# A written-out order per engine from step 31 on, and ten of the float64 tiles moved beside the attention

## The chip, the cores and the metric

One core of a Trainium2 chip. Times are device microseconds (us). The engines are called as the profile calls them: PE (TensorE, with its weight load PEld), DVE (VectorE), ACT (ScalarE), POOL (GpSimd) and SP (SyncE, which issues most transfers).

## What is computed

Landmark attention, then a gated layer, then a layer with PReLU (the reference, shortened; 576 positions, 8 heads of 64, batch 4, 32 landmarks):

```python
A, Bm, C = sm(q, k_lm), sm(q_lm, k_lm), sm(q_lm, k)      # softmax; _lm: means of 18 rows
Z = Bm.transpose(0, 1, 3, 2) / (norm1(Bm) * norminf(Bm) + 1e-06)
for _ in range(6):
    Z = 2 * Z - Z @ Bm @ Z
x = (A @ Z @ C @ v)                                      # as 2304 tokens x 512
x = (sigmoid(x @ w_gate) * (x @ w_val)) @ w_out          # 512 -> 1536 -> 512
h = x @ w_in2
out = (maximum(h, 0) + alpha * minimum(h, 0)) @ w_out2   # 512 -> 2048 -> 512
```

The weights come as float64. The kernel turns them into float32 on the chip.

## The kernel before

**Products.** A float32 product is made of three matmuls: each factor is split into a rounded high part and the remainder (`split`: a cast on ACT, L129, and a subtraction, L130, on DVE, or on POOL where asked for).

**The gated layer** runs in 96 steps, `at = 24*b + i`, over batches b, halves of 288 tokens and the 12 slices f of 128 of the 1536 features. A step first issues `layer1`: 12 matmuls into two banks `gv` (L716), a sigmoid on ACT (L727), a multiplication on DVE (L728), and the split of the result into `gs` (cast L129, subtraction L130). Then it issues `layer2` (L735, 12 matmuls into four banks `acc`) of the step two before it (`LAG`, `catch_up`). After the last f of a half the four banks are copied out (`xs`, L928) and stored to `x2d`. The attention of batches 1 to 3 is cut into pieces (`later_attentions`) that are issued between these steps, and its result is folded into the weights (`fold`, steps 19 to 55); those of batch 3 are stored (`we3d`) and fetched again by `take_stored`, two at every second step from step 61 on, through two buffers `st`.

**Float64 tiles.** The weights of the last layer are 32 tiles of 128 x 512 float64 (512 KB). `narrow_w2` loads one into `raw2` and makes float32 of it by integer operations on its halves: `scale` on ACT (L154), then `low` on ACT (L158, even tiles) or a shift on DVE (L160, odd tiles), then two joins on DVE (L163, L166), of which the second writes the tile `n2`; that is stored to `w2d`. From step 53 on it is called once per 0.9 step (`NARROW_EVERY`). There are two `raw2` buffers and one `n2` buffer. The first two tiles run early; 30 run in the steps from 57 on.

**The final stage** follows step 95: pairs of seven products (`prod`, L1024) and the output layer (`o`, L1068). Its inputs are `x7`, made from `x2d` by `load_x`, `sums_x` (L849) and `make_x7`. For the first group of tokens eight parts of them are issued together at step 74 and six at step 83 (`X2_AT`).

**What sets the order.** Each engine runs its own queue in order. The order of a queue is made ahead of time from the order in which the code issues operations, with priorities (`tc.high_priority`), by a scheduler. Nothing in the kernel before fixes it by hand, except `behind_of`, which puts one instruction behind another in this ordering.

Of the kernel before, what the change touches and what calls it, by code (L numbers as in the profile page):

```python
# [21 lines left out]
def tile_landmark_attention_glu_prelu(  # L22
# [45 lines left out]
    X2_AT, W2_AT = (74, 83), (88, 91)  # L68
# [7 lines left out]
    NARROW_FROM, NARROW_EVERY = 53, 0.9  # L76
# [58 lines left out]
    narrowed = [None]  # L135

# [7 lines left out]

    def raw_tile(name):
        return wpool.tile([P, NW], U64, tag="raw", name=name, bufs=4)

    def narrow(raw, to=None, act=False):
# [17 lines left out]
        narrowed[0] = nc.vector.scalar_tensor_tensor(  # L166
# [3 lines left out]
        return w[:, :, 0]  # L170
# [536 lines left out]
    def layer1(b, half, f):  # L707
# [19 lines left out]
        nc.scalar.activation(g, pss[0][:, :HB], AF.Sigmoid)  # L727
        nc.vector.tensor_tensor(out=g, in0=g, in1=pss[1][:, :HB], op=ALU.mult)  # L728
        split(gs, g)
# [71 lines left out]
    def narrow_w2(i):  # L801

        f, which = divmod(i, 2)
        pool = rpool or apool
        raw = pool.tile([P, NW], U64, tag="raw2", name="raw2", bufs=2)
        if which == 0:
            nc.sync.dma_start(
                out=raw.rearrange("p (a c) -> p a c", a=NK),
                in_=w_in2[:, P * f : P * f + P].rearrange("(a p) c -> p a c", p=P),
            )  # L810
        else:
            nc.sync.dma_start(out=raw, in_=w_out2[P * f : P * f + P, :])
        t = pool.tile([P, NW], F32, tag="n2", name="n2", bufs=1)
        narrow(raw, t, act=which == 0)
# [33 lines left out]
    def sub(out, x, y):  # L848
        nc.vector.tensor_tensor(out=out, in0=x, in1=y, op=ALU.subtract)  # L849

    def sums_x(i):
        b11, b12, b22, t1, t2 = (xf[i][n] for n in ((0, 0), (0, 1), (1, 1), "T1", "T2"))
        sub(t1, b12, b11)
        sub(t2, b22, t1)

        sub(b12, b22, b12)

    def make_x7(i, op, kk):
        if i == 0 and (op, kk) == (6, 0):
            sums_x(i)  # L860
# [9 lines left out]
        split(t, src[:, kk])  # L870
# [29 lines left out]
    part = {}  # L900
    to_narrow = deque(range(2 * NF2))
# [5 lines left out]
    behind = deque()  # L907
# [24 lines left out]
    for b in range(B):  # L932
# [5 lines left out]
        for i, (half, f, f0, f1) in enumerate(order):  # L938
            at = 24 * b + i
            behind.append((b, half, f, f0, f1, layer1(b, half, f)))  # L940
# [47 lines left out]
            if at == X2_AT[1]:
                assert not to_narrow
# [174 lines left out]
```

## Time and profile before

| | |
|---|---|
| median of 3 runs | 871.6 us (867.6 to 872.51) |
| the profiled execution: its own time | 870.5 us |
| its span | 868.7 us |
| mean granted TensorE clock | 0.976 of full speed |
| PE busy | 814.9 us (94%), x6017 |
| PEld busy | 712.6 us (82%) |
| DVE busy | 579.4 us (67%), x1205 |
| ACT busy | 468.1 us (54%), x982 |
| POOL busy | 68.9 us (8%), x70 |

All stages together share one execution; the span is the time from its first to its last instruction, and the execution's own time adds what lies around it. The gated layer's steps take up the time to 483 us, the final stage the rest. A share of busy time is an average over stages with different limits, so the stretches are read apart below.

### The profile page before, as it was taken

The page shows a single profiled execution, that of the slowest core. Times are in us where ns is not written, and L with a number is a line of the kernel's source. Part 1 is how long each engine was busy: PE and PEld are TensorE (multiplying, and loading weights), DVE is VectorE, ACT ScalarE, POOL GpSimd, SP SyncE. Part 2 cuts the span into 40 slices and gives each one's busy share as a digit, 9 for nine tenths or more (in the row PEclk, how much of TensorE's full clock was granted, in tenths as well). Part 3 has the DMA queues.
Part 4 walks back from the last instruction along what each step waited for, and adds up shares of the span by engine and source line. Part 5 has one row for each costly group of instructions (what it writes and reads, how often), then busy time and mean ns, then how long its engine had stood idle before and what let it go on. Part 6 is the DMA issues. An engine that isn't in the chain of part 4 may idle for free.

```text
span 868.7 us, 15870 instructions
## 1 busy us (share of the span) xinstructions
PE 814.9 (94%) x6017; PEld 712.6 (82%) x6017; DVE 579.4 (67%) x1205; ACT 468.1 (54%) x982; POOL 68.9 (8%) x70
## 2 busy tenths in 40 slices
PE   5688889999999999987999899999999999999996
PEld 4366667777889878987999798988989989989895
DVE  2799998666573444778686788889554568645544
ACT  6766785466452344556454556556444356444443
POOL 0131223111110100340000000000000000000000
PEclk9779999999999999998999999999999999999999
DMA  9768787864312344777687464576643345652002
GB/s 251 260 198 242 237 270 212 226 179 124 79 42 98 126 145 149 244 248 252 228 246 243 174 242 146 197 246 216 189 135 112 104 147 182 203 185 98 1 1 72
DMA packets 98604, 150.99 MB, mean 174 GB/s; under 512 B 37328, under 2 KB 58336, under 8 KB 98528
## 3 DMA queue, kind: packets, MB, share of 16 engines
q1 hardware_dynamic: 95072, 137.40, 50.1%
q0 software_dynamic: 3456, 12.58, 4.6%
q8 instruction: 47, 0.77, 0.4%
q14 instruction: 29, 0.24, 0.1%
HBM read 108.01 MB, written 41.94 MB: 173 GB/s over the span
## 4 chain that ended last, share of the span: by engine, by line
PE 68%; DMA 10%; DVE 10%; ACT 5%; issue 4%; POOL 2%; SPq 1%; DVEq 0%; ACTq 0%; POOLq 0%
PE o L1068 23%; PE prod L1024 20%; PE gv L716 9%; PE acc L735 9%; DMA raw<-in_moe_w_in_dram 3%; DMA w2d<-n 2%; PE psf L675 2%; DVE raw L163 2%; PE psq L215 1%; DVE n L166 1%; DMA raw<-in_moe_w_out_dram 1%; ACT raw L158 1%; DMA raw<-in_moe_w_val_dram 1%; PE psc L238 1%; PE psa L238 1%
## 5 line engine op out<-in xcount | busy, mean ns | idle before, releaser
L1024 PE MATMUL prod<-x,w 128*128 128x384 f32 x1008 | 199.8, 337 | 1.6 <-ACT p L1092 1.6
L716 PE MATMUL gv<-A,we 128*128 128x288 f32 x1152 | 190.5, 308 | 10.5 <-DVE g L728 3.8
L1024 PEld LDWEIGHTS prod<-x,w 128*128 128x128 f32 x1008 | 180.3, 188 | 14.5 <-ACT p L1092 1.9
L716 PEld LDWEIGHTS gv<-A,we 128*128 128x128 f32 x1152 | 164.0, 193 | 32.8 <-issue 16.6
L735 PE MATMUL acc<-gs,wconv 128*128 128x288 f32 x1152 | 181.0, 302 | 9.8 <-DVE gs L130 4.8
L1068 PE MATMUL o<-w,g2s 128*128 128x512 f32 x693 | 180.4, 393 | 0.0
L735 PEld LDWEIGHTS acc<-gs,wconv 128*128 128x128 f32 x1152 | 162.1, 191 | 18.2 <-DVE gs L130 6.9
L1068 PEld LDWEIGHTS o<-w,g2s 128*128 128x128 f32 x693 | 128.3, 188 | 19.9 <-DVE g2s L130 0.3
L1038 ACT ACTIVATE n<-h 128x384 f32<-128x384 f32 x96 | 50.4, 525 | 90.8 <-DVE h L1085 90.0
L1040 DVE SCALAR_TENSOR_TENSOR h<-n,minus_alpha,h 128x384 f32<-128x384 f32 x96 | 59.1, 617 | 53.8 <-ACT h L1039 53.5
L129 ACT CAST gs<-g 128x288 fp32r<-128x288 f32 x96 | 41.3, 431 | 62.3 <-DVE g L728 61.8
L728 DVE TENSOR_TENSOR g<-g,gv 128x288 f32<-128x288 f32 x96 | 43.1, 449 | 32.7 <-PE gv L716 29.1
L129 ACT CAST g2s<-h 128x384 fp32r<-128x384 f32 x77 | 39.4, 513 | 44.9 <-DVE h L1040 44.9
L163 DVE SCALAR_TENSOR_TENSOR raw<-raw 128x512 uint32<-128x512 uint32 x68 | 52.0, 777 | 14.3 <-ACT raw L158 13.0
L727 ACT ACTIVATE g<-gv 128x288 f32<-128x288 f32 x96 | 39.3, 409 | 39.8 <-PE gv L716 38.9
L154 ACT ACTIVATE raw<-raw 128x512 f32<-128x512 f32 x68 | 45.8, 681 | 27.3 <-DMA raw<-in_moe_w_out_dram 12.2
L130 DVE TENSOR_TENSOR gs<-g,gs 128x288 fp32r<-128x288 f32 x96 | 47.3, 493 | 18.4 <-ACT gs L129 18.0
L1085 DVE TENSOR_TENSOR h<-u,prod 128x384 f32<-128x384 f32 x72 | 39.8, 553 | 26.1 <-PE prod L1024 22.9
L1039 ACT ACTIVATE h<-h 128x384 f32<-128x384 f32 x96 | 50.4, 525 | 2.7
L130 DVE TENSOR_TENSOR g2s<-h,g2s 128x384 fp32r<-128x384 f32 x77 | 42.7, 556 | 11.0 <-ACT g2s L129 9.4
L1068 PE MATMUL o<-w,g2r 128*128 128x512 f32 x171 | 45.2, 393 | 0.0
L1068 PEld LDWEIGHTS o<-w,g2r 128*128 128x128 f32 x171 | 31.7, 188 | 5.1
(160 smaller groups left out, 836.1 us busy)
## 6 DMA issues: line engine op xcount, KB each, us to landing
w<-w7d SPq DMA_DIRECT2D x48, 512.0 KB, 3.6
raw<-in_moe_w_out_dram SPq DMA_DIRECT2D x28, 512.0 KB, 5.2
wgv<-wgvd POOLq DMA_DIRECT2D x24, 512.0 KB, 4.5
w7d<-w SPq DMA_DIRECT2D x24, 512.0 KB, 3.0
raw<-in_moe_w_in_dram SPq DMA_DIRECT2D x16, 512.0 KB, 4.4
w2d<-n SPq DMA_DIRECT2D x32, 256.0 KB, 2.6
raw<-in_moe_w_gate_dram SPq DMA_DIRECT2D x24, 256.0 KB, 4.0
raw<-in_moe_w_val_dram SPq DMA_DIRECT2D x24, 256.0 KB, 4.4
```

What stands on the lines that cost most here:

```text
L129: nc.scalar.copy(dst[:, 0, :], src)
L130: (nc.gpsimd if lo == "pool" else nc.vector).tensor_tensor(out=dst[:, 1, :], in0=src, in1=f32(dst[:, 0, :]), op=ALU.subtract)
L154: nc.scalar.activation(w[:, :, 1], w[:, :, 1], AF.Copy, scale=2.0 ** -112)
L163: nc.vector.scalar_tensor_tensor(out=lo, in0=hi, scalar=0x80000000, in1=lo, op0=ALU.bitwise_and, op1=ALU.bitwise_or)
L716: nc.tensor.matmul(ps[:, :HB], lhsT=We[b, c, j][:, a, 256 * i + P * s : 256 * i + P * s + P], rhs=att[b, j, "A"][half][:, e, :], start=(n ...
L728: nc.vector.tensor_tensor(out=g, in0=g, in1=pss[1][:, :HB], op=ALU.mult)
L735: nc.tensor.matmul(acc[m][:, :HB], lhsT=wout_sb[f][:, a, P * m : P * m + P], rhs=gs[:, e, :], start=(f == f0 and n == 0), stop=(f == f1 - ...
L1024: nc.tensor.matmul(ps[:, :HG], lhsT=w[:, a, kk], rhs=x7[i, op, kk][:, e], start=(n == 0), stop=(n == 5),)
L1038: nc.scalar.activation(n, h, AF.Relu, scale=-1.0)
L1039: nc.scalar.activation(h, h, AF.Relu)
L1040: nc.vector.scalar_tensor_tensor(out=h, in0=n, scalar=minus_alpha[:, f : f + 1], in1=h, op0=ALU.mult, op1=ALU.add)
L1068: nc.tensor.matmul(acc, lhsT=gs[:, a, P * t : P * t + P], rhs=w2_out[f][:, e, :], start=(count[i, u] == 1 and k == 0), stop=(count[i, u] = ...
```

## The change

- Ten of the 30 tiles get places at steps 34, 36, ... 52, and 20 at steps 58, 59, 60, 62, ... 85 (`NARROW_AT`). The first two are made at step 30's place in the code, at a priority that puts them where they were.
- From step 31 on (`PIN_FROM`) `layer1` issues the operations of a step, those of the tile among them, in a written-out order, and `pin` puts each behind the one that was pinned before it on the same engine. That fixes the order in the queue and adds no wait. The order is: shift (odd tiles), sigmoid, scale, multiplication, cast, subtraction, low (even tiles), joins. The store of a tile and the load of a later one are issued one step after it, behind the subtraction.
- Buffers: from step 56 on three for `raw2` (one of its own, two of tag A) and two for `n2`.
- `we3` is fetched one per step at steps 58 to 69, and taken one per step (`load_stored`, `take_stored`).
- The parts of `x7` of the first group are made one per step, eight from step 75 and six from step 88, with the subtraction on POOL; the three sums of `xf` stand at steps 77, 78 and 79.

```diff
-    X2_AT, W2_AT = (74, 83), (88, 91)
+    X2_AT, W2_AT = (74, 87), (88, 91)
-    NARROW_FROM, NARROW_EVERY = 53, 0.9
+    NARROW_FROM, NARROW_AHEAD, PIN_FROM, PIN_POOL = 30, -2000, 31, 56
+    NARROW_AT = {*range(34, 53, 2), *(58 + 29 * i // 20 for i in range(20))}
+    def pin(ins):
+        e = ins.ins.engine
+        if e in pinned:
+            behind_of(ins, pinned[e])
+        pinned[e] = ins
+        return ins
-    def take_stored(c):
-        for j in range(2):
-            st = rpool.tile([P, NW], F32, tag="st3", name="st3", bufs=2)
-            nc.sync.dma_start(out=st, in_=we3d[c, j])
-            We[B - 1, c, j] = ws_tile("we3")
-            split(We[B - 1, c, j], st, lo="pool")
+    def load_stored(c, j):
+        st = rpool.tile([P, NW], F32, tag="st3", name="st3", bufs=2)
+        pin(nc.sync.dma_start(out=st, in_=we3d[c, j]))
+        stored.append((c, j, st))
+    def take_stored():
+        c, j, st = stored.popleft()
+        We[B - 1, c, j] = t = ws_tile("we3")
+        pin(nc.scalar.copy(t[:, 0, :], st))
+        nc.gpsimd.tensor_tensor(out=t[:, 1, :], in0=st, in1=f32(t[:, 0, :]), op=ALU.subtract)
...
+        tile_ = loaded.popleft() if at in NARROW_AT else None
+        if tile_ is not None and tile_[0] % 2:
+            pin(narrow_shift(tile_[1]))
+        pin(nc.scalar.activation(g, pss[0][:, :HB], AF.Sigmoid))
+        if tile_ is not None:
+            pin(narrow_scale(tile_[1]))
+        pin(nc.vector.tensor_tensor(out=g, in0=g, in1=pss[1][:, :HB], op=ALU.mult))
+        pin(nc.scalar.copy(gs[:, 0, :], g))
+        rest = pin(
+            nc.vector.tensor_tensor(
+                out=gs[:, 1, :], in0=g, in1=f32(gs[:, 0, :]), op=ALU.subtract
+            )
+        )
+        if to_store:
+            i, t = to_store.popleft()
+            load_w2(rest)
+            behind_of(pin(nc.sync.dma_start(out=w2d[i], in_=t)), rest)
+        if tile_ is not None:
+            i, raw = tile_
+            if i % 2 == 0:
+                pin(narrow_low(raw))
+            t = (rpool or apool).tile([P, NW], F32, tag="n2", name="n2", bufs=2 if rpool else 1)
+            for ins in narrow_join(raw, t):
+                pin(ins)
+            to_store.append((i, t))
...
+        if rpool is None:
+            raw = apool.tile([P, NW], U64, tag="raw2", name="raw2", bufs=2)
+        elif i % 3:
+            raw = bpool.tile([P, NW], U64, tag="A", name="raw2", bufs=4)
+        else:
+            raw = rpool.tile([P, NW], U64, tag="raw2", name="raw2", bufs=1)
...
-        split(t, src[:, kk])
+        note(nc.scalar.copy(t[:, 0, :], src[:, kk]))
+        note(
+            (nc.gpsimd if i == 0 else nc.vector).tensor_tensor(
+                out=t[:, 1, :], in0=src[:, kk], in1=f32(t[:, 0, :]), op=ALU.subtract
+            )
+        )
...
-            if at >= NARROW_FROM:
-                narrow_pace += 1 / NARROW_EVERY
-                while to_narrow and narrow_pace >= 1:
-                    narrow_w2(to_narrow.popleft())
-                    narrow_pace -= 1
+            if at in (PIN_FROM, PIN_POOL):
+                for _ in range(2 if at == PIN_FROM else 3):
+                    load_w2(pinned[mybir.EngineType.DVE])
             if at == X2_AT[0]:
                 load_x(0)
-                for op, kk in PARTS7[:8]:
-                    make_x7(0, op, kk)
+                x2_todo = deque(PARTS7[:8])
+            elif x2_todo:
+                op, kk = x2_todo.popleft()
+                if op in (2, 6) and (op, kk) != (6, 1):
+                    pin(sum_x(0, 2 * (op == 6) + kk))
+                make_x7(0, op, kk, pin)
```

The order of DVE's queue at step 34, where the attention of batches 2 and 3 runs (`kT`, `qT`: its keys and queries; `psa`, `ta`: its scores). Before:

```order
L728 TENSOR_TENSOR g<-g,gv_3270 128x288
L130 TENSOR_TENSOR gs<-g,gs 128x288
L221 TENSOR_REDUCE kT_3298<-kT_3298 128x32
L221 TENSOR_REDUCE qT_3313<-qT_3313 128x32
L388 STREAM_TRANSPOSE ta<-psa_3358 128x512
```

The same place of the changed kernel (L770 is the multiplication, L773 the subtraction, L183 and L185 are the joins):

```order
L770 TENSOR_TENSOR g<-g,gv_3290 128x288
L773 TENSOR_TENSOR gs<-g,gs 128x288
L183 SCALAR_TENSOR_TENSOR raw_3130<-raw_3130 128x512
L185 SCALAR_TENSOR_TENSOR n_3305<-raw_3130 128x512
L246 TENSOR_REDUCE kT_3323<-kT_3323 128x32
L246 TENSOR_REDUCE qT_3338<-qT_3338 128x32
L413 STREAM_TRANSPOSE ta<-psa_3386 128x512
```

The two joins of a tile now stand between the step's subtraction and the reduction of kT.

DVE's queue at step 36, at the start of the Newton iterations that run there (`srz`, `psz`: its matrices; `cv`, `at`, `A`: the attention beside it). Before:

```order
L416 STREAM_TRANSPOSE at<-ta 128x576
L516 TENSOR_TENSOR srz<-sbt 128x4x32
L130 TENSOR_TENSOR gs<-g,gs 128x288
L130 TENSOR_TENSOR A_3534<-at,A_3534 128x288
L511 TENSOR_TENSOR srz<-psbb,sbt 128x4x32
L130 TENSOR_TENSOR A_3537<-at,A_3537 128x288
L512 TENSOR_TENSOR srz<-eye,srz 128x4x32
L361 TENSOR_SCALAR cv<-psv,rd 128x64
L529 TENSOR_TENSOR srz<-srz,psz 128x4x32
```

The changed kernel:

```order
L773 TENSOR_TENSOR gs<-g,gs 128x288
L541 TENSOR_TENSOR srz<-sbt 128x4x32
L183 SCALAR_TENSOR_TENSOR raw_3132<-raw_3132 128x512
L441 STREAM_TRANSPOSE at<-ta 128x576
L536 TENSOR_TENSOR srz<-psbb,sbt 128x4x32
L185 SCALAR_TENSOR_TENSOR n_3451<-raw_3132 128x512
L537 TENSOR_TENSOR srz<-eye,srz 128x4x32
L386 TENSOR_SCALAR cv<-psv,rd 128x64
L131 TENSOR_TENSOR A_3570<-at,A_3570 128x288
L131 TENSOR_TENSOR A_3573<-at,A_3573 128x288
L554 TENSOR_TENSOR srz<-srz,psz 128x4x32
```

The two joins stand inside the chain of srz, the tile's shift some rows ahead of these, and the two subtractions for A have moved behind it. On PE the first psz group of this chain, which stood behind three matmuls of a gv group, now stands behind seven.

ACT's queue at steps 66 to 68 (L727 sigmoid, L129 cast, L154 scale, L158 low). Before:

```order
L727 ACTIVATE g<-gv_5007 128x288
L129 CAST gs<-g 128x288
L154 ACTIVATE raw_4815<-raw_4815 128x512
L129 CAST we_5171<-st_5169 128x512
L727 ACTIVATE g<-gv_5047 128x288
L129 CAST gs<-g 128x288
L154 ACTIVATE raw_4859<-raw_4859 128x512
L158 ACTIVATE raw_4859<-raw_4859 128x512
L129 CAST we_5176<-st_5174 128x512
L727 ACTIVATE g<-gv_5097 128x288
```

The changed kernel (L767 sigmoid, L771 cast, L165 scale, L170 low, L733 the cast of `we3`):

```order
L767 ACTIVATE g<-gv_5046 128x288
L165 ACTIVATE raw_4940<-raw_4940 128x512
L771 CAST gs<-g 128x288
L170 ACTIVATE raw_4940<-raw_4940 128x512
L733 CAST we_5086<-st_5002 128x512
L767 ACTIVATE g<-gv_5091 128x288
L771 CAST gs<-g 128x288
L733 CAST we_5126<-st_5044 128x512
L767 ACTIVATE g<-gv_5131 128x288
L165 ACTIVATE raw_4984<-raw_4984 128x512
```

Scale has moved ahead of its step's cast, and not every step has one.

## Rows read from the trace of the kernel before

**Rows 1.** PE timeline, undisturbed: start us, length us, engine, line, operation, out<-in, count
```profile
416.80 1.74 PE L716 MATMUL gv<-A,we 128*128 128x288 f32 x12
418.38 1.75 PE L735 MATMUL acc<-gs,wconv 128*128 128x288 f32 x12
```

**Rows 2.** PE timeline, step 57 to the first prod; in brackets idle time before, its releaser
```profile
340.17 1.74 PE L716 MATMUL gv<-A,we 128*128 128x288 f32 x12
...
405.06 1.49 PE L735 MATMUL acc<-gs,wconv 128*128 128x288 f32 x9 [2.55 <-ACT xs L928]
...
408.11 3.08 PE L716 MATMUL gv<-A,we 128*128 128x288 f32 x12
...
481.57 1.86 PE L735 MATMUL acc<-gs,wconv 128*128 128x288 f32 x12 [0.42 <-DVE gs L130]
...
483.26 2.25 PE L1024 MATMUL prod<-x,w 128*128 128x384 f32 x12
```

**Rows 3.** Windows: span, busy us of PE, PEld, DVE, ACT, POOL, PEclk, DMA share, GB/s
```profile
230.00:285.00 55.00, 54.07 (x723) 49.48 (x722) 28.77 (x85) 24.18 (x60) 5.66 (x7) 1.00 0.22 66
285.00:340.00 55.00, 55.00 (x498) 42.97 (x498) 23.78 (x46) 21.28 (x46) 2.64 (x5) 1.00 0.37 123
340.00:483.00 143.00, 133.81 (x961) 130.50 (x960) 104.55 (x198) 76.95 (x167) 17.34 (x12) 0.98 0.75 243
374.00:414.00 40.00, 33.12 (x209) 30.76 (x208) 31.51 (x56) 21.85 (x48) 8.56 (x6) 0.91 0.79 250
```

**Rows 4.** Waits, 340 to 483: us in total, times, longest us
```profile
ACT raw L154 <- DMA raw<-in_moe_w_out_dram: 12.2, 8, 3.1
ACT raw L154 <- DMA raw<-in_moe_w_in_dram: 11.0, 9, 3.1
...
DVE n L166 <- DMA w2d<-n: 5.5, 9, 1.2
```

**Rows 5.** ACT timeline at one late load
```profile
392.54 0.68 ACT L154 ACTIVATE raw<-raw 128x512 f32<-128x512 f32 x1 [3.12 <-DMA raw<-in_moe_w_in_dram]
...
393.66 0.39 ACT L727 ACTIVATE g<-gv 128x288 f32<-128x288 f32 x1
...
394.88 0.43 ACT L129 CAST gs<-g 128x288 fp32r<-128x288 f32 x1 [0.82 <-DVE g L728]
```

**Rows 6.** Lines, 340 to 483: count, busy us, mean ns, idle before
```profile
L158 ACT ACTIVATE raw<-raw 128x512 uint32<-128x512 uint16 x15 | 9.9, 658 | 0.0
...
L160 DVE TENSOR_SCALAR raw<-raw 128x512 uint32<-128x512 uint32 x15 | 6.4, 425 | 7.0 <-DMA raw<-in_moe_w_out_dram 7.0
...
L129 ACT CAST we<-st 128x512 fp32r<-128x512 f32 x12 | 7.4, 627 | 2.6 <-DMA st<-we3d 2.4 <-PE gv L716 0.2
...
L130 POOL TENSOR_TENSOR we<-st,we 128x512 fp32r<-128x512 f32 x12 | 17.3, 1459 | 61.7 <-ACT we L129 57.0 <-PE acc L735 4.7
...
L849 DVE TENSOR_TENSOR xf<-xf 128x768 f32<-128x768 f32 x4 | 3.8, 950 | 0.0
```

**Rows 7.** DMA issues, 340 to 480: KB each, median us to landing
```profile
raw<-in_moe_w_in_dram SPq DMA_DIRECT2D x14, 512.0 KB, 4.4
...
st<-we3d SPq DMA_DIRECT2D x12, 256.0 KB, 3.7
```

**Rows 8.** POOL and DVE timelines while POOL runs and behind it
```profile
384.04 2.98 POOL L130 TENSOR_TENSOR we<-st,we 128x512 fp32r<-128x512 f32 x2 [3.11 <-ACT we L129]
...
384.31 0.46 DVE L728 TENSOR_TENSOR g<-g,gv 128x288 f32<-128x288 f32 x1
...
385.81 1.52 DVE L130 TENSOR_TENSOR gs<-g,gs 128x288 fp32r<-128x288 f32 x1
...
387.77 0.69 DVE L163 SCALAR_TENSOR_TENSOR raw<-raw 128x512 uint32<-128x512 uint32 x1
```

**Rows 9.** DVE timeline at step 34
```profile
242.40 0.46 DVE L130 TENSOR_TENSOR gs<-g,gs 128x288 fp32r<-128x288 f32 x1 [0.50 <-ACT gs L129]
243.98 0.75 DVE L221 TENSOR_REDUCE kT<-kT 128x32 f32<-128x576 f32 x1 [1.12 <-ACT kT L220]
```

More of the change, by code (lines that the diff above doesn't have):

```diff
@@ L169, in narrow @@
         )
-        return w[:, :, 0]
+    def narrow(raw, to=None, act=False):
+        narrow_scale(raw)
+        (narrow_low if act else narrow_shift)(raw)
+        narrowed[0] = narrow_join(raw, to)[1]
+        return words(raw)[0][:, :, 0]
     att = {}
@@ L726, in layer1 @@
         gs = bpool.tile([P, 2, HB], F32R, tag="gs", name="gs", bufs=GS_BUFS)
[L727 to L729 removed]
+        if at < PIN_FROM:
+            nc.scalar.activation(g, pss[0][:, :HB], AF.Sigmoid)
+            nc.vector.tensor_tensor(out=g, in0=g, in1=pss[1][:, :HB], op=ALU.mult)
+            split(gs, g)
+            return gs
+        tile_ = loaded.popleft() if at in NARROW_AT else None
[23 more added lines that the diff above has]
+            to_store.append((i, t))
         return gs
@@ L799, in make_w2_out, with load_w2 @@
             split(w2_out[2 * g + i], t[:, i])
-    def narrow_w2(i):
-        f, which = divmod(i, 2)
-        pool = rpool or apool
-        raw = pool.tile([P, NW], U64, tag="raw2", name="raw2", bufs=2)
+    loaded, to_store = deque(), deque()
+    def load_w2(after=None):
+        if not to_narrow or (rpool is None and after is not None and to_narrow[0] >= EARLY):
+            return
+        i = to_narrow.popleft()
+        f, which = divmod(i, 2)
+        if rpool is None:
[4 more added lines that the diff above has]
+            raw = rpool.tile([P, NW], U64, tag="raw2", name="raw2", bufs=1)
         if which == 0:
-            nc.sync.dma_start(
+            ins = nc.sync.dma_start(
                 out=raw.rearrange("p (a c) -> p a c", a=NK),
@@ L811, in narrow_w2 @@
         else:
-            nc.sync.dma_start(out=raw, in_=w_out2[P * f : P * f + P, :])
-        t = pool.tile([P, NW], F32, tag="n2", name="n2", bufs=1)
-        narrow(raw, t, act=which == 0)
+            ins = nc.sync.dma_start(out=raw, in_=w_out2[P * f : P * f + P, :])
+        if after is not None:
+            behind_of(pin(ins), after)
+        loaded.append((i, raw))
+    def narrow_w2():
+        load_w2()
+        i, raw = loaded.pop()
+        t = apool.tile([P, NW], F32, tag="n2", name="n2", bufs=1)
+        narrow(raw, t, act=i % 2 == 0)
         nc.sync.dma_start(out=w2d[i], in_=t)
@@ L848, in sub, with sum_x, make_x7 @@
     def sub(out, x, y):
-        nc.vector.tensor_tensor(out=out, in0=x, in1=y, op=ALU.subtract)
+        return nc.vector.tensor_tensor(out=out, in0=x, in1=y, op=ALU.subtract)
+    def sum_x(i, n):
+        b11, b12, b22, t1, t2 = (xf[i][m] for m in ((0, 0), (0, 1), (1, 1), "T1", "T2"))
+        return sub(*((t1, b12, b11), (t2, b22, t1), (b12, b22, b12))[n])
     def sums_x(i):
[L852 to L860, printed above, removed]
+        for n in range(3):
+            sum_x(i, n)
+    def make_x7(i, op, kk, note=lambda ins: ins):
         b11, b12, b21, b22, t1, t2 = (
@@ L900, in tile_landmark_attention_glu_prelu @@
     part = {}
+    EARLY = 12
     to_narrow = deque(range(2 * NF2))
@@ L906, in tile_landmark_attention_glu_prelu @@
     accs = {}
-    behind = deque()
+    behind, x2_todo = deque(), None
     def catch_up():
@@ L939, in tile_landmark_attention_glu_prelu @@
             at = 24 * b + i
-            behind.append((b, half, f, f0, f1, layer1(b, half, f)))
+            behind.append((b, half, f, f0, f1, layer1(at, b, half, f)))
             if len(behind) > LAG:
```

53 lines of the change are left out of this document (33 added, 20 removed).

## The prediction

> **What bounds the kernel now.** I read the busy shares first: TensorE (PE) is at work for 94% of the span, so only what makes PE wait can move the time. Next I took PE's timeline where nothing disturbs it [rows 1]: a step is one gv group and one acc group of 12 matmuls, and groups start 1.58 to 1.59 us apart, so a step takes 3.17 us. Then I took the stretch from gv of step 57, at 340.17, to the first prod of the final stage, at 483.26 [rows 2]: 143.1 us for 39 gv groups and 41 acc groups (468 and 493 records of 12 each). At 1.585 us each they need 80 x 1.585 = 126.8. So **16.3 us are lost there**, and that is the ceiling of any gain in this stretch. Rows 2 show the kind of loss: acc waits 2.55 us at 405.06 (the four acc banks are copied out late, because the engines that copy are late), and .42 for gs at 481.57. Soon behind the wait of 405 a gv group takes 3.08 us instead of 1.74; the granted clock over 374 to 414 is 0.91 [rows 3], so part of the time is paid after the wait, at PE's lower level of 1.2 GHz.
>
> Who is late? The table of waits [rows 4]: ScalarE (ACT) stands at L154, the first operation on a float64 tile, for 12.2 + 11.0 us, for the two kinds of loads, and VectorE (DVE) at L166 for 5.5 us until the single n2 buffer is stored. ACT runs in order, so its queue stands with it: at 392.54 it waits 3.12 us for raw, and the sigmoid L727 starts only at 393.66, behind scale and low [rows 5]. The reason is the pace: 30 tiles are asked for every 0.9 step (2.85 us), while a load takes 4.4 us to land [rows 7] and there are two buffers for it.
>
> Last I looked for room. From 285 to 340 PE is busy 55.00 of 55.00 us, DVE 23.8 and ACT 21.3; from 230 to 285 it is 54.07, 28.8 and 24.2 [rows 3]. So beside the attention DVE has 57 us free of 110.
>
> **The change, part by part.**
>
> *Ten tiles move to steps 34 to 52.* A tile costs ACT .68 (scale) and, if even, .66 (low); DVE .42 (shift) if odd, and two joins. The durations are in rows 5 and 6, and a join that nothing stretches takes .69 [rows 8]. Ten tiles: DVE 20 x .69 + 5 x .42 = 15.9 us, ACT 10 x .68 + 5 x .66 = 10.1. Cover: DVE 57 us free, ACT 110 - 45.5 = 64 [rows 3]. Their loads have room too (DMA share .22 and .37). So in bulk they cost nothing. If that cover did not exist, each tile would put 2.6 us on PE's path (the last rival).
>
> They do stand in fixed places. At step 34 the two joins now stand ahead of the kT reduce. Before, gs ends its subtraction at 242.40 + .46 and the reduce starts at 243.98 [rows 9]. The cast ends by 242.40, low (.66) by 243.06, two joins (1.38) by 244.44, so the reduce is about .4 late, and PE's next psa products with it. At step 36 two joins and a shift (1.80) stand inside the Newton chain, and two subtractions of A (.92) moved behind it, and PE does four matmuls more of gv in between (.53): 1.80 - .92 - .53 = .35 (a matmul is 1.585 / 12 = .132). The other eight tiles meet fewer attention operations; I estimate .45 for them together. Sum **+1.2**; bounds 0 (PE has gv matmuls to fill with) and 3.9 (the same stalls, with the clock's lower level behind them for two groups, as at 408: 2 x (3.08 - 1.74) = 2.7 more).
>
> *Twenty tiles over steps 58 to 85.* One per 1.45 steps, 4.6 us. With a landing of 4.4 [rows 7] and three raw buffers, a load leaves at the latest behind the next step's subtraction and is first used two to three steps later: 6.34 us allowed, so 1.9 to spare. Two n2 buffers: a store has 1.45 steps more than the old one, which cost 5.5 us of DVE waits. Per step DVE has at most .46 + .46 + 1.38 + .42 = 2.72 us, ACT .41 + .68 + .43 + .66 + .63 = 2.81, both under 3.17 (mult and gs in rows 8 and 9, sigmoid and cast in rows 5, we3's cast in rows 6). So no engine is over its step, on average or at worst.
>
> *Fixed order.* Sigmoid now stands ahead of scale, so a late tile no longer delays g; it delays the cast behind it. From the start of a gv group gs is ready after 1.59 (the group) + .3 + .46 (multiplication) + .5 + .46 (subtraction), about 3.3 us, the .3 and .5 being as the idles of rows 9; the acc group that reads it runs two steps later and starts 5 groups after, at 7.92. **Slack 4.6 us** per step. All the single waits on raw of rows 4 are at most 3.1 long: such a wait, if it came, would be swallowed.
>
> *we3 one per step* (before, two at every second step): cast .63 [rows 6], POOL subtraction 1.46, landing 3.7 [rows 7], 5.8 us around two buffers that are asked for every two steps, 6.34. It fits by .5.
>
> *x7 of group 0: eight parts at steps 75 to 82 and six at 88 to 93, one each, subtraction on POOL (GpSimd) instead of DVE.* Fourteen subtractions leave DVE. But rows 8 show what POOL does to DVE: while POOL runs, from 384.04 to 387.02, the subtraction for gs takes 1.52 us instead of the .46 of rows 9, while the multiplication, one of whose inputs is in PSUM, keeps its .46. So I price a POOL instruction at 1.52 - .46 = 1.06 us of DVE (high, if anything: the one in rows 8 has 512 columns, a part of x7 has 384). At steps 75 to 82 DVE needs 8 x (.46 + .46) for mult and gs, 6 x 1.38 for joins, 3 x .42 for shifts and 3 x .95 for the sums of x [rows 6]: 19.7. With 8 x 1.06 = 8.5 it is 28.2, against 8 x 3.17 = 25.4. That is 2.8 over, less than the slack of 4.6, so I take **0**; bounds 0 and 2.8 (no slack left).
> The Trainium skill, page "SBUF — State Buffer", section "Who interferes with whom", speaks against this part of the change: a DVE instruction with two inputs in SBUF and a GpSimd instruction that reads SBUF share a port pair, and the one that comes second is blocked for the whole of the other. Rows 8 agree (gs +1.06, the PSUM multiplication +0). By that rule DVE could stand for each POOL instruction's whole 1.46 us: 8 x 1.46 = 11.7 and 6.0 over, 1.4 past the slack, and the sum would be 1.4 higher.
>
> *What stays.* Two gs waits at the end, of which rows 2 show the second, .42: nothing fills in after step 95, -.8. Three x2d evictions of acc (at steps where a half ends) need ACT and DVE twice each in one step: I estimate .4 each, -1.2, the size of that gs wait (the one at 405.06 is 2.55 now, with ACT late).
>
> Sum: 16.3 - .8 - 1.2 = 14.3 back, 1.2 given for the ten tiles: 13.1. Against the profiled execution's own 870.5 us that is 857.4; the median of before is 871.6, 1.1 above it, so half of that on top: **858**.
>
> **Rivals.**
>
> *Half of it comes back.* The loads land later than 4.4 now that stores, st and raw loads stand in one fixed SP queue. If the st loop takes landing 6, it is 8.1 against 6.34: 1.8 late on each of 6 rounds = 10.5, less one slack of 4.6 = 6 lost: 864. For: the DMA share of .75 in 340 to 483, where it is .37 ahead of it [rows 3]. Against: the same bytes over a longer time (ten tiles are gone from it). 861 to 866.
>
> *All of it comes back*, and the ten tiles cost nothing: 870.5 - 16.3 = 854.2. For: the ten tiles' DVE time is free. Against: the last gs waits have nothing to hide behind.
>
> *The port decides.* The slack is used up by late loads when steps 75 to 82 come, and all 2.8 us show: 857.4 + 2.8, about 861 with the median's offset. For: rows 8. Against: the slack is 4.6, and late loads would first have to use 1.8 of it. (The Trainium skill's rule above would make this 6.0 instead of 2.8, so 864.)
>
> *Moved, not hidden.* If the ten tiles' DVE work delays attention chains that PE waits for, 15.9 us are paid in steps 34 to 52 instead: 870.5 - 14.3 + 15.9 = 872, no change. Against: 57 us of free DVE time.
>
> *Slower.* Both DVE and ACT work of each tile (.68 + .66 + 1.38 or .68 + .42 + 1.38, 2.6 us on average) lands on the chain that PE follows, 10 x 2.6 = 26: 870.5 - 14.3 + 26 = 882. It decides from about 1.4 us per tile (14.3 / 10) for slower than before at all, and 1.9 for measurably. For: step 36 stands in the Newton chain, which is serial. Against: [rows 3], PE 54.07 of 55 busy there, so it hardly ever waits, and other matmuls are ready.
>
> **How the numbers follow.** Forecast (854.5 to 860) .55; all back .07; half .17; port .08; no change .08; slower .05. The predicted time is 858. A range of 853.5 to 866 holds the first four, .87; it takes in the bounds 0 and 3.9 of the ten tiles and 2.8 of the port. A run of this kernel tells 0.5% apart, 4.3 us: faster is below 867.2, slower above 876. Faster .87, same .08, slower .05.
>
> **What would show it.** Steps of 3.17 us from 58 to 95; first prod 143.1 - 14.3 = 128.8 us after gv of step 57; waits of ACT at the scale under 5 us in all; no wait of acc over 1 us; granted clock 1.0 in that stretch; PE idle at steps 34 to 38 up by about 1 us. I am wrong if the scale still waits for raw over 10 us, if st or POOL is the last releaser of gv, or if steps 34 to 52 take more than 4 us longer.

## The result, and the profile after

The changed kernel takes 856.1 us (median of 4 runs, 853.16 to 856.62) against 872.06 (4 runs, 867.6 to 873.22): ratio 0.983, interval 0.981 to 0.986. The forecast was 858, with a range of 853.5 to 866. The profiled execution took 856.62 us, its span is 854.8, so it stands 13.9 us under the one of before.

PE's timeline of the changed kernel at the places of [rows 2] (columns as there):

```profile
343.42 1.74 PE L747 MATMUL gv<-A,we 128*128 128x288 f32 x12
...
464.20 1.75 PE L747 MATMUL gv<-A,we 128*128 128x288 f32 x12
465.79 4.93 PE L794 MATMUL acc<-gs,wconv 128*128 128x288 f32 x36
470.55 2.25 PE L1113 MATMUL prod<-x,w 128*128 128x384 f32 x12
473.43 4.43 PE L1113 MATMUL prod<-x,w 128*128 128x384 f32 x24 [0.63 <-ACT p L1181]
```

From gv of step 57 to the first prod it is now 470.55 - 343.42 = **127.1 us**, where it was 143.1 and the work alone is 126.8. No step from 57 to 94 takes longer than 3.22 us, and the last three acc groups stand in one row of 36 matmuls without a gap: the gs waits of 481.57 have gone. The first wait behind it is .63 us, for p.

The windows of the two stretches beside the attention and of this stretch (columns as in [rows 3]):

```profile
233.00:288.00 55.00, 53.62 (x717) 48.58 (x717) 35.54 (x96) 28.11 (x65) 5.86 (x7) 1.00 0.42 123
288.00:343.40 55.40, 55.40 (x501) 43.37 (x501) 31.16 (x58) 25.22 (x53) 2.64 (x5) 1.00 0.57 189
343.40:470.50 127.10, 127.10 (x962) 127.10 (x961) 93.36 (x168) 72.17 (x158) 33.68 (x26) 1.00 0.70 230
```

Beside the attention DVE does 66.7 us instead of 52.6 (35.54 + 31.16 against 28.77 + 23.78), 14 more, close to the 15.9 reckoned, and PE remains busy (53.62 of 55, and all of the next window). In the last window PE never stops, at full clock.

The waits there (columns as in [rows 4]):

```profile
ACT gs L771 <- DVE g L770: 29.5, 32, 3.1
...
ACT we L733 <- DMA st<-we3d: 3.2, 5, 1.5
...
```

There is no row of ACT at the scale (L165) any more; it was 23.2 us in two rows of [rows 4]. In the first row ACT waits for the multiplication of the step; PE waits for nothing in this stretch. Lines in the same stretch (columns as in [rows 6]):

```profile
L185 DVE SCALAR_TENSOR_TENSOR n<-raw 128x512 uint32<-128x512 uint32 x20 | 23.0, 1148 | 0.6
L773 DVE TENSOR_TENSOR gs<-g,gs 128x288 fp32r<-128x288 f32 x40 | 18.4, 459 | 15.9 <-ACT gs L771 15.6
...
L948 POOL TENSOR_TENSOR x<-xf,x 128x384 fp32r<-128x384 f32 x14 | 17.0, 1217 | 49.0 <-ACT x L946 42.2 <-DVE gs L773 6.8
...
L734 POOL TENSOR_TENSOR we<-st,we 128x512 fp32r<-128x512 f32 x12 | 16.7, 1388 | 65.1 <-ACT we L733 64.8 <-DVE gs L773 0.4
...
L165 ACT ACTIVATE raw<-raw 128x512 f32<-128x512 f32 x20 | 13.4, 670 | 0.0
```

Scale has no idle time before it (0.0). The second join (L185) takes 1148 ns on average, where one undisturbed takes 690: the collision with POOL falls on it, not on the subtraction for gs (459).

**Where 13.9 us come from.** Stretch 57 to prod: 143.1 - 127.1 = 16.0 back. The first pair of the final stage is 12.3 us instead of 13.5 (482.89 - 470.55 against 496.77 - 483.26): 1.2 back. Steps 31 to 44 take 61.35 instead of 60.68: .7 given. Gv of step 31 starts 2.6 us later (226.06 against 223.47), ahead of the first tile that was moved: given too, but the last experiment finds 3.9 us between two executions of one kernel there, so it is within chance. 16.0 + 1.2 - .7 - 2.6 = 13.9.

### The profile page after: what moved, and what is told of

Same layout as the page of the kernel before. It is cut to its first block, busy times and chain, and to the rows that moved or that the text cites. A ratio compares the mean times of both kernels' runs of the same rounds, so it can differ in the third digit from the quotient of the medians.

```text
span 854.8 us, 15852 instructions
## 1 busy us (share of the span) xinstructions
PE 809.7 (95%) x6017; PEld 710.7 (83%) x6017; DVE 580.0 (68%) x1191; ACT 469.9 (55%) x982; POOL 85.2 (10%) x84
## 4 chain that ended last, share of the span: by engine, by line
PE 80%; DVE 8%; DMA 4%; ACT 3%; issue 2%; POOL 2%; SPq 1%; POOLq 0%; DVEq 0%; ACTq 0%
PE o L1157 23%; PE prod L1113 21%; PE acc L794 14%; PE gv L747 14%; PE psf L700 2%; DVE raw L183 2%; PE psq L240 2%; DMA raw<-in_moe_w_val_dram 1%; PE psc L263 1%; PE psa L263 1%; DMA tk<-in_k_dram 1%; DMA tkT<-in_k_dram 1%; PE psz L504 1%; DVE wgv L185 1%; DMA raw<-in_moe_w_out_dram 1%
## 5 line engine op out<-in xcount | busy, mean ns | idle before, releaser
L747 PE MATMUL gv<-A,we 128*128 128x288 f32 x1152 | 188.6, 306 | 8.6 <-DVE g L760 2.9
L794 PE MATMUL acc<-gs,wconv 128*128 128x288 f32 x1152 | 178.1, 300 | 2.7 <-DVE gs L131 2.4
L183 DVE SCALAR_TENSOR_TENSOR raw<-raw 128x512 uint32<-128x512 uint32 x68 | 50.6, 755 | 1.8
L771 ACT CAST gs<-g 128x288 fp32r<-128x288 f32 x65 | 28.1, 432 | 42.8 <-DVE g L770 42.8
L165 ACT ACTIVATE raw<-raw 128x512 f32<-128x512 f32 x68 | 45.5, 675 | 5.6 <-DMA raw<-in_moe_w_val_dram 2.4
L770 DVE TENSOR_TENSOR g<-g,gv 128x288 f32<-128x288 f32 x65 | 29.2, 449 | 28.5 <-PE gv L747 27.0
L773 DVE TENSOR_TENSOR gs<-g,gs 128x288 fp32r<-128x288 f32 x65 | 29.8, 458 | 25.6 <-ACT gs L771 25.3
L767 ACT ACTIVATE g<-gv 128x288 f32<-128x288 f32 x65 | 26.6, 409 | 34.3 <-PE gv L747 34.1
```

The lines of the kernel that those rows point to most:

```text
L165: return nc.scalar.activation(w[:, :, 1], w[:, :, 1], AF.Copy, scale=2.0 ** -112)
L183: return nc.vector.scalar_tensor_tensor(out=lo, in0=hi, scalar=0x80000000, in1=lo, op0=ALU.bitwise_and, op1=ALU.bitwise_or), nc.vector.sca ...
L747: nc.tensor.matmul(ps[:, :HB], lhsT=We[b, c, j][:, a, 256 * i + P * s : 256 * i + P * s + P], rhs=att[b, j, "A"][half][:, e, :], start=(n ...
L794: nc.tensor.matmul(acc[m][:, :HB], lhsT=wout_sb[f][:, a, P * m : P * m + P], rhs=gs[:, e, :], start=(f == f0 and n == 0), stop=(f == f1 - ...
```

## The experiments

All times below named "the stretch" are those from gv of step 57 to the first prod in a profile of that kernel: before 143.1, changed 127.1, work 126.8. A time of a run differs by some us from one execution to the next, mostly ahead of step 31; the stretch does not (127.13 in both profiles of the changed kernel).

**One tile per step, none beside the attention.**

```diff
-    NARROW_FROM, NARROW_AHEAD, PIN_FROM, PIN_POOL = 30, -2000, 31, 56
-    NARROW_AT = {*range(34, 53, 2), *(58 + 29 * i // 20 for i in range(20))}
+    NARROW_FROM, NARROW_AHEAD, PIN_FROM, PIN_POOL = 30, -2000, 31, 55
+    NARROW_AT = {*range(57, 87)}
...
-    EARLY = 12
+    EARLY = 2
```

> The changed kernel with its written-out order, but no tile beside the attention: 30 tiles, one at every step from 57 to 86 (loads start at step 55). Theory A (pace: what was lost was lost because tiles were asked for faster than loads land, 2.85 us against 4.4): at 3.17 us a tile the loads are late again, ACT or DVE waits for raw more than 5 us in all, and the stretch from gv of step 57 to the first prod takes 133 to 140 us (before 143.1, after 127.1): 862 to 869. Theory B (order: it was lost because the sigmoid stood behind a waiting scale): the stretch stays within 2 us of after's 127.1, about 856 less 1 for the attention steps that carry no tile.

Measured: stretch 140.1, 869.6 us, ratio to before 1.000 (0.998 to 1.002). With a tile at every step the rest of the change brings 3.0 us of the stretch, and nothing that the timed runs can tell. That lies just past theory A's ranges, but not for its reason. The waits in its stretch (columns as in [rows 4]):

```profile
DVE n L185 <- DMA w2d<-n: 7.4, 8, 3.0
...
PE gv L747 <- DVE g L770: 5.5, 7, 2.0
...
ACT raw L165 <- DMA raw<-in_moe_w_out_dram: 3.3, 2, 2.7
...
ACT raw L165 <- DMA raw<-in_moe_w_in_dram: 0.7, 3, 0.3
```

The loads are nearly in time: ACT waits 4.0 us for raw, where it was 23.2 us before, although the tiles are asked for almost as fast (one per step, before one per 0.9). Now DVE is late. Here are two steps of its timeline:

```profile
385.87 0.44 DVE L770 TENSOR_TENSOR g<-g,gv 128x288 f32<-128x288 f32 x1
386.81 0.46 DVE L773 TENSOR_TENSOR gs<-g,gs 128x288 fp32r<-128x288 f32 x1 [0.50 <-ACT gs L771]
387.19 0.69 DVE L183 SCALAR_TENSOR_TENSOR raw<-raw 128x512 uint32<-128x512 uint32 x1
387.91 1.67 DVE L185 SCALAR_TENSOR_TENSOR n<-raw 128x512 uint32<-128x512 uint32 x1
389.50 0.44 DVE L770 TENSOR_TENSOR g<-g,gv 128x288 f32<-128x288 f32 x1
390.44 0.46 DVE L773 TENSOR_TENSOR gs<-g,gs 128x288 fp32r<-128x288 f32 x1 [0.50 <-ACT gs L771]
391.02 0.69 DVE L183 SCALAR_TENSOR_TENSOR raw<-raw 128x512 uint32<-128x512 uint32 x1
391.75 1.67 DVE L185 SCALAR_TENSOR_TENSOR n<-raw 128x512 uint32<-128x512 uint32 x1
393.33 0.42 DVE L176 TENSOR_SCALAR raw<-raw 128x512 uint32<-128x512 uint32 x1
393.67 0.44 DVE L770 TENSOR_TENSOR g<-g,gv 128x288 f32<-128x288 f32 x1
```

POOL's timeline at the same time:

```profile
387.38 1.65 POOL L734 TENSOR_TENSOR we<-st,we 128x512 fp32r<-128x512 f32 x1 [2.31 <-ACT we L733]
391.57 1.29 POOL L734 TENSOR_TENSOR we<-st,we 128x512 fp32r<-128x512 f32 x1 [2.54 <-ACT we L733]
```

From one multiplication (389.50) to the next (393.67) DVE takes 4.17 us in a step that has a join under a POOL subtraction and the shift of the next tile, and 3.63 without that shift (385.87 to 389.50), against PE's 3.17. Of it .50 is an idle that the fixed order makes (DVE waits for ACT's cast with nothing else to do), and 1.67 - .69 = .98 is the join that stands beside POOL.

**The same, with POOL only writing.**

```diff
-        nc.gpsimd.tensor_tensor(out=t[:, 1, :], in0=st, in1=f32(t[:, 0, :]), op=ALU.subtract)
+        nc.gpsimd.memset(f32(t[:, 1, :]), 0.0)
```

The same stands for the x7 parts of group 0.

> The one-per-step kernel with POOL's 26 subtractions (12 of we3, 14 of x7 of group 0) replaced by a memset to zero on POOL, which reads nothing from SBUF; it leaves out the low parts of these products. Port theory (in the one-per-step kernel DVE needs .44 + .50 + .46 + .69 + 1.67 = 3.76 us in a step with a tile and a POOL subtraction, over the 3.17 that PE takes): without the stretch it needs 3.0 and the loss of 13.3 us against 126.8 goes to under 4: 57 to first prod 127 to 131 us. Load or store theory (tiles come or go too slowly at one per step): it stays at 137 to 141.

Measured: stretch 132.3, 859.1 us, ratio 0.986 (0.984 to 0.988), which lies between the two theories and nearer the first. In the lines of its stretch the second join is short again:

```profile
L185 DVE SCALAR_TENSOR_TENSOR n<-raw 128x512 uint32<-128x512 uint32 x30 | 20.8, 693 | 13.6 <-DMA w2d<-n 13.0
...
L734 POOL MEMSET we<- 128x512 f32 x9 | 4.6, 534 | 38.0 <-PE gv L747 32.6 <-DVE g L770 5.4
```

So 7.8 of the 13.3 us lost at one tile per step go with POOL's subtractions. The memset is also shorter than the subtraction (.53 against 1.50), and it stands at other times, because it waits for no cast; what each of these did is not apart. But four of the second joins in this stretch had .24 to .69 us of a memset beside them, and each took .69, so a POOL instruction that only writes did not stretch them. The remaining 5.5 us go with waits for transfers: 13.0 us of the join for the store of n2, and 6.5 us of scale for its loads, to which a tile per step leaves too little time. Neither was taken away by itself.

**Ten tiles early, the 20 later ones one per step.**

```diff
-    NARROW_AT = {*range(34, 53, 2), *(58 + 29 * i // 20 for i in range(20))}
+    NARROW_AT = {*range(34, 53, 2), *range(58, 78)}
```

> The changed kernel with its ten tiles beside the attention, but the 20 later ones at every step from 58 to 77 instead of over 58 to 85. DVE reckoning: twelve steps with a we3 subtraction on POOL and three with one of x7 each need about .67 more than 3.17, 10 us, less the slack of 4.6: some 5 lost, 57 to first prod 130 to 134, 859 to 863. If only the number of tiles in the stretch counts (20 against 30): 127 to 128, as in the change.

Measured: stretch 134.5, 863.4 us, ratio 0.992 (0.990 to 0.995), just past the range of the DVE reckoning. Nearly all of the loss (7.5 of 7.7) lies in steps 69 to 75. By then DVE's arrears (how much later than usual gs is ready) have used up the slack. Its steps beside a POOL subtraction run 3.6 to 4.2 us there too, and gs is ready 3.3 us after its gv starts at step 60, and 10.0 us at step 69, where the acc group that reads it would start after 7.9. In the changed kernel it is never later than 5.9. The number of tiles in the stretch is that of the change; what it lacks are the steps without one.

**No order by hand.**

```diff
     def pin(ins):
-        e = ins.ins.engine
-        if e in pinned:
-            behind_of(ins, pinned[e])
-        pinned[e] = ins
+        pinned[ins.ins.engine] = ins
         return ins
```

> The changed kernel without the ordering by hand (pin orders nothing); places, buffers, x7 and we3 as in the changed kernel. Theory A (pace): 57 to first prod 127 to 130 us, 856 to 859. Theory B (order): waits for raw stand ahead of sigmoids again, 133 to 140 us, 862 to 869.

Only the loads and stores of the tiles still stand behind the subtraction of their step here.

Measured: stretch 133.1, 863.8 us, ratio 0.994 (0.991 to 0.996): 6.0 us of the 16 are lost again, at three steps, 62 (2.4), 69 (1.2) and 74 (2.4). DVE's timeline ahead of the first of these:

```profile
350.40 0.61 DVE L770 TENSOR_TENSOR gs<-g,gs 128x288 fp32r<-128x288 f32 x1 [0.50 <-ACT gs L768]
352.90 2.03 DVE L922 TENSOR_TENSOR xf<-xf 128x768 f32<-128x768 f32 x1 [1.89 <-POOL x L945]
354.85 0.44 DVE L767 TENSOR_TENSOR g<-g,gv 128x288 f32<-128x288 f32 x1
```

POOL's timeline there:

```profile
350.87 2.00 POOL L945 TENSOR_TENSOR x<-xf,x 128x384 fp32r<-128x384 f32 x2 [0.17 <-ACT x L943]
```

PE's timeline at step 62:

```profile
359.85 1.62 PE L791 MATMUL acc<-gs,wconv 128*128 128x288 f32 x9 [1.70 <-DVE xs L1007]
```

A sum of xf (L922), which the code issues at step 77, has been put at step 60, ahead of a step's multiplication: it waits 1.89 us for POOL's x7 and then takes 2.03 instead of .95. That step's multiplication comes 3.3 us behind its sigmoid (which ends at 351.5), and with it the copies that acc waits 1.70 for at step 62. The rows of such waits in its stretch (columns as in [rows 4]):

```profile
ACT we L730 <- DMA st<-we3d: 3.4, 3, 2.3
...
DVE xf L922 <- POOL x L945: 2.9, 2, 1.9
```

At step 74 it is a sum of xf again, which waits 1.06 us for POOL's x7 and then takes 1.75. At step 69 it is ACT: the cast of a we3 part waits 2.34 us for st (at 380.75), and the cast of gs stands behind it. Theory B's numbers came true, its reason only in part: ACT waits 8.1 us for raw again, none of it at steps 60 to 62 or 74; what these waits add to the arrears at step 69 is not apart. The order's worth is that all such work stays in its place. The ten early tiles stayed near their places (steps 33 to 52), and steps 31 to 44 took 60.60 us, though nothing but their loads and stores was put in order.

**Scale ahead of the sigmoid, in the fixed order.**

```diff
+        if tile_ is not None:
+            pin(narrow_scale(tile_[1]))
+            if tile_[0] % 2 == 0:
+                pin(narrow_low(tile_[1]))
         pin(nc.scalar.activation(g, pss[0][:, :HB], AF.Sigmoid))
-        if tile_ is not None:
-            pin(narrow_scale(tile_[1]))
...
-            if i % 2 == 0:
-                pin(narrow_low(raw))
```

> The changed kernel with scale (and low) of a tile ahead of the sigmoid of its step, as near to the old queue as the fixed order allows. Theory A: the loads are in time, ACT waits for none (0 us on raw after the change), so the sigmoid is later by .68 or 1.34 us of a slack of 4.6, and nothing is lost: 855 to 858. Theory B: sigmoid behind scale costs again, over 861.

Measured: stretch 128.1, 855.4 us, ratio 0.985 (0.981 to 0.988). Which of the two is first is worth .9 us at most, as long as the loads are in time.

**Only the places.** The kernel before, with the two first tiles called at step 30, the others at the new steps, and the second part of x7 at step 87; buffers, we3 and x7 as before.

```diff
-    X2_AT, W2_AT = (74, 83), (88, 91)
+    X2_AT, W2_AT = (74, 87), (88, 91)
...
-    NARROW_FROM, NARROW_EVERY = 53, 0.9
+    NARROW_AT = {*range(34, 53, 2), *(58 + 29 * i // 20 for i in range(20))}
...
-            if at >= NARROW_FROM:
-                narrow_pace += 1 / NARROW_EVERY
-                while to_narrow and narrow_pace >= 1:
-                    narrow_w2(to_narrow.popleft())
-                    narrow_pace -= 1
+            if at == 30:
+                narrow_w2(to_narrow.popleft())
+                narrow_w2(to_narrow.popleft())
+            if at in NARROW_AT:
+                narrow_w2(to_narrow.popleft())
```

> The kernel before with nothing but the tiles' places changed (ten at steps 34 to 52, 20 at steps 58 to 85, each called where it stands; two raw buffers, one n2 buffer, x7 parts together at steps 74 and 87, we3 in pairs, no order by hand). Theory A (pace alone suffices): 57 to first prod under 132 us, 856 to 862. Theory B: over 136 us, 864 to 872. A burst theory (x7 parts together at step 74 cost 4 to 6 us there): a loss of 4 to 6 us at steps 74 to 76 and little elsewhere.

Measured: stretch 136.3, so 6.8 of the 16 us come back there; but 872.0 us, ratio 1.001 (0.998 to 1.004), which are theory B's numbers. Gv of step 25 starts at 200.34 instead of 188.36. Of these 12.0 us, 7.9 lie in steps 20 to 24, so the gain is paid in front; 4.1 lie ahead of step 16, before any of the moved tiles is loaded. The line of the second join up to 260 us (columns as in [rows 6]):

```profile
L166 DVE SCALAR_TENSOR_TENSOR n<-raw 128x512 uint32<-128x512 uint32 x12 | 8.2, 680 | 5.2 <-DMA w2d<-n 5.1
```

Twelve tiles are done by then; before it were two (x2 in that line). Nothing held the ten early ones at their steps: their second joins stand at steps 19 to 35, seven of them ahead of step 30, where nothing had been reckoned for them.

The slower pace did not take the waits for the loads away. The rows of the scale in its stretch (columns as in [rows 4]):

```profile
ACT raw L154 <- DMA raw<-in_moe_w_out_dram: 11.0, 6, 2.7
...
ACT raw L154 <- DMA raw<-in_moe_w_in_dram: 10.3, 6, 3.4
```

These are 21.3 us, against 23.2 before, with 20 tiles at the places of the changed kernel; of what bears on the loads, this kernel lacks the third buffer, their place behind the subtraction and the order.

**we3 in pairs, in the fixed order.**

```diff
-            if len(stored) > 1 or (stored and b > 2):
-                take_stored()
-            if 58 <= at < 70:
-                load_stored(*divmod(at - 58, 2))
+            if b == 2 and half and f % 2:
+                for j in range(2):
+                    load_stored(f // 2, j)
+                    take_stored()
```

> The changed kernel with the stored we3 parts fetched and taken in pairs at every second step from 61 on, as before (in the written-out order). If the pairs made the loss of 5.8 us at steps 67 to 71 before: 3 to 6 us lost there, 57 to first prod 130 to 133. If the tiles' pace and order did: under 1 us more than the change, 127 to 128.5.

Measured: stretch 146.3, 877.5 us, ratio 1.006 (1.004 to 1.009): slower than before, and a miss of both expectations. ACT's timeline at one of the pairs:

```profile
361.01 1.27 ACT L733 CAST we<-st 128x512 fp32r<-128x512 f32 x2 [6.77 <-DMA st<-we3d]
362.18 0.40 ACT L767 ACTIVATE g<-gv 128x288 f32<-128x288 f32 x1
```

The row of the waits in its stretch (columns as in [rows 4]):

```profile
ACT we L733 <- DMA st<-we3d: 20.9, 5, 6.8
```

The cast of a part stands in the fixed order right behind its load, so ACT waits 6.77 us for it, the sigmoid L767 too, which stands behind it, and the like at other pairs: 20.9 us in five waits. What this undoes is both the pairing and the fetch one step ahead, and the row shows the second.

**x7's subtractions on DVE; x7's parts together.**

```diff
-            (nc.gpsimd if i == 0 else nc.vector).tensor_tensor(
+            nc.vector.tensor_tensor(
```

> The changed kernel with the subtractions for the fourteen x7 parts of group 0 on DVE again (one part per step as in the change). The port theory (a POOL subtraction lengthens the join beside it by about its own length, so DVE has .55 us of its own work in place of about 1 us of stretch): no loss, 57 to first prod 127 to 129 us, 855 to 858. A theory that the move to POOL was what brought the gain: 131 us or more, over 860.

The second of these kernels also makes the eight parts together at step 74 and the six at step 87, outside the written-out order.

> The changed kernel with the x7 parts of group 0 made together, eight at step 74 and six at step 87, on DVE, with no place in the written-out order (as in the kernel before). The burst theory (this is what cost 4.18 and 2.35 us after steps 74 and 75 before): 4 to 6 us lost there, 57 to first prod 131 to 134. The pace theory: DVE has some 7 us of work at once, which the slack of 4.6 and the free time of the next steps take up, under 2 us lost.

Measured: stretch 127.1 in both; 856.6 us, ratio 0.983 (0.980 to 0.986), and 856.4, 0.985 (0.982 to 0.987). Neither the move to POOL nor the spreading of x7 had a part in the gain. The burst of eight costs nothing here, but the queue put it at steps 77 to 79 (DVE's subtractions from 407.8 to 414 us; two other parts and a sum of xf ran at step 60, without loss), while before it ran at steps 74 to 76, where the acc banks of a half are copied out. What it would cost there without arrears was not run. That the 4.18 us lost at step 74 before needed the arrears is likely, since the one-per-step kernel loses 2.2 there without a burst.

No run takes the third buffer of raw or the second of n2 away by itself.

**The ten tiles from step 38 on, and the changed kernel again.**

```diff
-    NARROW_AT = {*range(34, 53, 2), *(58 + 29 * i // 20 for i in range(20))}
+    NARROW_AT = {*(38 + 17 * i // 10 for i in range(10)), *(58 + 29 * i // 20 for i in range(20))}
```

> The changed kernel with the ten early tiles at steps 38, 39, 41, 43, 44, 46, 48, 49, 51 and 53 instead of 34 to 52, so that none stands beside the reductions of step 34 and the Newton chain of step 36. If these two places make the .67 us that steps 31 to 44 are longer in the change (61.35 against 60.68): 60.6 to 60.9 there, and 0.5 less in all, which the timed runs can't tell. If the load on DVE as such makes it: 61.3 again.

> The changed kernel once more beside the others on the same chip: 855 to 857.5; a second profile shows how much of the 2.1 us that steps 25 to 31 took longer (a wait for a load of keys, ahead of the change's first instruction) belongs to one execution: theory of chance, 35 to 36.5 us for steps 25 to 31 instead of 37.2.

Measured: steps 31 to 44 take 60.68 us without the tiles at 34 and 36, exactly what they took before, and 61.30 in the changed kernel again. The .67 are those two places. In time: 853.9 us, ratio 0.981 (0.979 to 0.984), against 856.3, 0.984 (0.982 to 0.986); the intervals overlap, so the timed runs do not tell the two apart.

Steps 25 to 31 took 35.11 us before, 37.18 in the first profile of the changed kernel and 33.26 in this one, below the 35 to 36.5 that were expected. PE's timeline in the first profile of the changed kernel:

```profile
220.31 1.20 PE L240 MATMUL psq<-ident,tkT 96*128 96x96 f32 x6 [2.92 <-DMA tkT<-in_k_dram]
...
222.31 3.08 PE L794 MATMUL acc<-gs,wconv 128*128 128x288 f32 x12
```

The same place in its second profile:

```profile
219.54 0.69 PE L240 MATMUL psq<-ident,tkT 96*128 96x96 f32 x6 [1.64 <-DMA tkT<-in_k_dram]
...
220.61 1.79 PE L794 MATMUL acc<-gs,wconv 128*128 128x288 f32 x12
```

PE waits for a load of keys, 2.92 us in one execution and 1.64 in the other, and the acc group behind the longer wait runs at the lower clock (granted .50 over its 3.08 us, and 1.00 over the 1.79 of the other). None of the moved tiles has been loaded by then, and it is one kernel both times: chance, 3.9 us of it.

## Why the prediction was right, and where not

**The ceiling and the gain.** That the stretch held 16.3 us of loss was right: 16.0 came back, 14.3 had been reckoned. The step that was mis-sized is "what stays": .8 for the last gs waits and 1.2 for three evictions, 2.0 us, of which .3 stayed. By the prediction's own numbers the gs of step 95 is ready 3.3 us after its gv starts and is needed 3 x 1.585 = 4.75 after it, so nothing had to wait. In the kernel before, the gs of steps 94 and 95 were ready 6.9 and 6.0 us after their gv started. At step 93 ACT had stood 3.13 us for the load of the last tile, and four parts of x7 came right behind it. ACT's timeline there:

```profile
470.04 0.68 ACT L154 ACTIVATE raw<-raw 128x512 f32<-128x512 f32 x1 [3.13 <-DMA raw<-in_moe_w_out_dram]
```

Added to that, 1.2 at the first pair had not been seen: before, p waits 3.1 us for a buffer that is being stored to x2d, and in the change it does not. Why that store came late is open; the kernel without the order has its last gs in time, and p waits 3.0 us there all the same.

For the profiled execution the forecast came as near as it did partly by luck: it had 13.1 us less and 13.9 were measured, but without the 2.6 us ahead of step 31 it would have been 16.5. The medians differ by 16.0.

**The cost of the ten tiles.** 1.2 us were forecast, .67 measured, and at the two places named. At step 34 the reduction starts behind the joins; DVE's timeline of the changed kernel:

```profile
245.00 0.46 DVE L773 TENSOR_TENSOR gs<-g,gs 128x288 fp32r<-128x288 f32 x1 [0.50 <-ACT gs L771]
245.59 0.69 DVE L183 SCALAR_TENSOR_TENSOR raw<-raw 128x512 uint32<-128x512 uint32 x1
246.31 0.69 DVE L185 SCALAR_TENSOR_TENSOR n<-raw 128x512 uint32<-128x512 uint32 x1
246.92 0.75 DVE L246 TENSOR_REDUCE kT<-kT 128x32 f32<-128x576 f32 x1
```

It starts at 246.92. The subtraction for gs stands 2.60 us later than in [rows 9] (245.00 against 242.40), so the reduction would have started at 243.98 + 2.60 = 246.58: it is .34 late, and step 35 is .33 longer (.4 reckoned). Step 37, behind the Newton chain, is .43 longer (.35 reckoned). The .45 for the other eight tiles was nothing.

**The mechanism.** That ACT stood for late loads in the kernel before was right, and these waits are gone. But three steps of the reasoning failed, though they did not move the sum. First, "The reason is the pace": with the places of the change but two raw buffers and no order (the only-the-places kernel) ACT still waits 21.3 us for raw, and at one tile per step with the third buffer, the loads behind the subtraction and the order it waits 4.0. So buffers, place of the loads and order took these waits away, and which of them did most is open.

Second, "no engine is over its step, on average or at worst": DVE takes 3.6 to 4.2 us in a step with a join beside a POOL subtraction, where 2.72 had been reckoned at most, since I left out the .50 of idle that the order makes and counted POOL's interference only for x7, not for we3's twelve parts. With a tile in 20 of 28 steps the others give it back; with one in each (the one-per-step kernel) 13.3 of 16.3 us are lost. So the pace of 1.45 steps does matter, but because of DVE and the transfers that a tile per step leaves too little time. The slack of 4.6 us per step, which I did count, is what carries the arrears.

Third, I gave the order's worth to the sigmoid standing ahead of scale. That is worth .9 us at most while the loads are in time. The order as a whole is worth 6.0 us in this stretch: without it a sum of xf that is ready early and a cast of we3 that is not ready yet stand ahead of a step's chain. And in the only-the-places kernel nothing kept the ten tiles beside the later attention.

**The landing times.** The rival of late loads was nearer than I thought. The DMA issues of the changed kernel in the stretch (columns as in [rows 7]):

```profile
w2d<-n SPq DMA_DIRECT2D x20, 256.0 KB, 4.4
raw<-in_moe_w_out_dram SPq DMA_DIRECT2D x9, 512.0 KB, 5.1
raw<-in_moe_w_in_dram SPq DMA_DIRECT2D x8, 512.0 KB, 4.7
...
st<-we3d SPq DMA_DIRECT2D x12, 256.0 KB, 4.3
```

A load of raw lands in 5.1 and 4.7 us (4.4 in [rows 7]), one of st in 4.3 (3.7). The st loop then takes 6.3 of its 6.34 us, and its cast did wait 3.2 us in all. The raw loop had been given 1.9 us to spare, and .3 to .7 of that went.

**The port.** The Trainium skill's rule (page "SBUF — State Buffer", section "Who interferes with whom") says that a DVE instruction with two inputs in SBUF contends with a GpSimd instruction that reads SBUF, not with one that only writes it, and that who issues first decides who is blocked. It holds in these traces: a join that starts behind a POOL subtraction takes up to 1.8 us (1.67 in the rows of the one-per-step kernel) instead of .69, one that starts just ahead of it takes .69 (at 376.48 in the changed kernel, with POOL starting at 376.59), and one beside a POOL instruction that only writes takes .69. The collision fell on the join, not on the subtraction for gs that the prediction named. For x7 it cost nothing, as forecast: 127.1 on either engine. Gs is ready at most 5.9 us after its gv starts (step 80) instead of 3.3, so 2.6 us of the slack went, where 2.8 had been reckoned.

**Rivals.** The rival that came nearest is "All of it comes back": 16.0 of 16.3 did. What was held against it, that the last gs waits have nothing to hide behind, was the term mis-sized above; its free ten tiles cost .67. "Moved, not hidden" and "slower" needed PE to follow the ten tiles; PE lost .67 us there. The only-the-places kernel ended at the 872 of "moved, not hidden", but by other terms: it paid 7.9 us at steps 20 to 24, not 15.9 at steps 34 to 52.

## What to carry to other kernels

Spread optional work so that the slowest engine's step, with its stretched instructions and the idles of a fixed order counted in, is below the bound engine's step on average, and check that the arrears of a run of full steps stay under the slack. A place in the code is no place in the queue: where a scheduler may move work that is ready early, it takes an order by hand to keep it out of the chain. A wait for a load need not come from the pace: look first at how many buffers it has and how far ahead it is issued. In a fixed order a transfer has to be issued a landing time ahead of its reader, or the whole queue waits with it.

## What the runs showed of the hardware

The same wait for a load of keys was 1.64 to 2.92 us in different executions of one kernel, and with the lower clock behind it steps 25 to 31 took 33.3 to 37.2 us; a difference of 4 us between two single profiles says nothing here. The lower of PE's two levels stood behind the longer of these waits (granted .50 over 3.08 us); in the stretch without any wait of PE 1.00 was granted over all 127.1 us.
